# Exponent logs stacked as high and low parts on 64 contraction rows, and another round list, in an S4 block with a gated feed-forward layer

## The chip, the cores and the metric

The kernel runs on one core of one Trainium2 chip. The metric is the device time of one execution in microseconds. All numbers of the profile come from one profiled execution of the kernel before; "PE" is TensorE, "PEld" its weight loads, "ACT" ScalarE, "DVE" VectorE, "POOL" GpSimd, "SP" SyncE, which here only issues transfers.

## The reference

One layer with adaptive normalisation, of L = 2048 positions and D = 640 channels, all in float32: a state-space convolution (S4, 128 complex states per channel), then a gated feed-forward layer of width 1728.

```python
x = A_u
sa, ca, ga, sb, cb, gb = six parts of (_silu(c) @ w_mod)
h = _layernorm(x) * (1 + ca) + sa
# S4: K[d, l] = Re sum_n C[d,n] * exp(dt[d] * A[d,n] * l) * dt[d] * B[d,n],  l = 0 .. 2047
# y = causal convolution of h with K along l (by FFT of length 2 L), + h * Dskip
x = x + ga * y
h = _layernorm(x) * (1 + cb) + sb
x = x + gb * ((_silu(h @ w1) * (h @ w3)) @ w2)
```

The change is in the making of K. The exponential of a complex number times l is split: its size is exp(Re(log) * l), its direction a cosine and a sine of a phase.

## The kernel before

The convolution half takes the first 420 us or so, the feed-forward half the rest. The change touches only the convolution half, which runs in *steps* of 16 channels (40 steps, `SD = 16`). A step s goes through these parts; the names in quotes are those of the round list:

- "PH", POOL: the phases of the step, integers, one pass of 128x1024 and one of 128x512 (`ph`, L472 and L473).
- "AB", "CO", "SI", ScalarE: the absolute value of the phase (`cs<-ph`), its cosine (`cs<-cs`) and sine (`ph<-ph`), 128x1024 each.
- "PA", TensorE: the exponents Re(log) * l for the fast table, made as a matmul (`pa`, L432). The stationary side is the transposed table of logs, the moving side a constant (`r2`) that holds l in the column of its channel. 32 rows of contraction hold 32 channels; a step needs two such blocks of rows, each one matmul of 128x512 into its own PSUM bank. The product must be exact to float32, but the operands are float32r, so the table is split in a high part (`lah`) and a low part (`lal`) and two matmuls are summed: 4 a step.
- "XA", ScalarE: Exp of `pa` into the table `A` (128x1024).
- "PQ", TensorE: the same for the slow table (`pq`, L444, 128x256): `lah` and `lal` against `r1`, and the logs of the amplitude (`lmh`, `lml`) against a selection `sel`, summed: 8 a step.
- "XQ", ScalarE: Exp of `pq` into `A` (128x512).
- "E1", "E2", "A1", "A2", VectorE: exponentials times cosines (into `E`) and times sines (in `A`).
- "kg", TensorE: the kernel K of the step (`pk`, 32 small matmuls); "K", VectorE: its copy with the gate; "pt", TensorE: the first stage of its Fourier transform; "uk", ScalarE: the copy of that.

The convolution follows ten steps behind (`LAG = 10`), in chunks of 128 channels: "st", TensorE: the second stage (`p2`, shown as `p`); "kc", ScalarE: a copy of half of it; "T" and "Y", VectorE: products and sums; "iv", TensorE: the inverse stage (`pz`); "zt", ScalarE, every second step: its copy, followed by two stores from SyncE.

Three stretches set the order differently. In the *lead-in* (steps 0 to 9, with the first normalisation and the first transform of the input between them) a scheduler orders the instructions; the exponents of two steps are made in one call, `exps(s)`, and `polar` makes the tables of logs, for the first 128 channels at the start and for the other 512 during the lead-in. In the *rounds* the order is written out by hand: `ROUND` lists parts with an offset, each turn of it does four steps, and every instruction is kept in program order on its engine. `do` skips what is done already or out of range. In the rounds `pa` and `pq` share the one PSUM place "B", of one buffer. The *drain* (from `st` of step 43 on) is in program order of a plain loop.

Of the kernel before, what the change touches and what calls it, by code (L numbers as in the profile page):

```python
# [29 lines left out]
KD = D // P  # L30
# [77 lines left out]
def tile_kernel(ctx: ExitStack, tc: tile.TileContext, a):  # L108
# [9 lines left out]
    ident = cp.tile([P, P], F32, name="ident")  # L118
# [18 lines left out]
    def acopy(out, in_):  # L137
        return tc.keep_in_program_order(S.copy(out, in_))  # L138
# [31 lines left out]
    once = lambda shape, dt, name: tp.tile(shape, dt, name=name, bufs=1)  # L170
    thi = once([P, D], I32, "thi")
    phi = once([P, D], I32, "phi")
    lah = once([P, KD, P], F32R, "lah")
    lal = once([P, KD, P], F32R, "lal")
    lmh = once([P, KD, P], F32R, "lmh")
    lml = once([P, KD, P], F32R, "lml")
    r2 = once([P, NA, NB], F32R, "r2")
    r1 = once([P, NA, NA], F32R, "r1")
    sel = once([P, NA], F32R, "sel")
# [57 lines left out]
    def polar(cs, E):  # L237

        are, aim, br, bi, cr, ci = (prm[:, i, cs] for i in range(6))
        ld, dtc, m, t, g_r, g_i = (v[:, cs] for v in (ldt, dt, m0, t3, gr, gi))  # L240
        k0, nk = cs.start // P, (cs.stop - cs.start) // P

        E.tensor_tensor(g_r, br, cr, op=OP.mult)
        E.tensor_tensor(m, bi, ci, op=OP.mult)
        E.tensor_tensor(g_r, g_r, m, op=OP.subtract)
        V.tensor_tensor(g_i, br, ci, op=OP.mult)
        V.tensor_tensor(t, bi, cr, op=OP.mult)
        V.tensor_tensor(g_i, g_i, t, op=OP.add)
# [24 lines left out]

        nat = lambda v: v.rearrange("n (k p r j) -> n k r p j", k=nk, p=4, r=4)
        rows = lambda v: v[:, :nk * P].rearrange("n (k r p j) -> n k r p j", k=nk, p=4, r=4)
        for k in range(nk):
            E.tensor_tensor(rows(lt[:, 0])[:, k], nat(are)[:, k], nat(dtc)[:, k], op=OP.mult)
        for k in range(nk):
            V.tensor_tensor(rows(lt[:, 1])[:, k], nat(q)[:, k], nat(ld)[:, k], op=OP.add)
        for i, (hi, lo) in enumerate(((lah, lal), (lmh, lml))):  # L280
            pT = psS.tile([P, 2, 512], F32, name="pT", tag="AB"[i], bufs=1)
            for k in range(nk):
                PE.transpose(pT[:, 0, k * P:(k + 1) * P], lt[:, i, k * P:(k + 1) * P], ident)
            pv = pT[:, 0, :nk * P].rearrange("p (k n) -> p k n", k=nk)
            acopy(hi[:, k0:k0 + nk], pv)
            V.tensor_tensor(lo[:, k0:k0 + nk], pv, hi[:, k0:k0 + nk].bitcast(F32), op=OP.subtract)

        V.tensor_scalar(m, m, 0.5 / math.pi, 0.125, op0=OP.mult, op1=OP.add)
        V.tensor_tensor(m, m, ag, op=OP.mult)
        V.scalar_tensor_tensor(m, m, 0.25, ai, op0=OP.add, op1=OP.mult)  # L290
        V.tensor_scalar(phi[:, cs], m, TURN, 2147483520.0, op0=OP.mult, op1=OP.min)
# [124 lines left out]
    ph, cs, AA, EC, PK, K1 = {}, {}, {}, {}, {}, {}  # L416

    def exp_rows(s):
        return s // SPC, slice((s % SPC) // 2 * 8, (s % SPC) // 2 * 8 + 8), [
            (rr, slice((2 * (s % 2) + rr) * 32, (2 * (s % 2) + rr) * 32 + 32)) for rr in range(2)]  # L420

    pA, pQ = {}, {}

    def exp_fast(steps):

        for s in steps:
            pA[s] = psS.tile([P, 2, 512], F32, name="pa", tag="AB"[s % 2] if not in_order[0] else "B", bufs=1)
        for w, st in ((lah, True), (lal, False)):
            for s in steps:
                ch, js, rows = exp_rows(s)  # L430
                for rr, r in rows:
                    keep(PE.matmul(pA[s][:, rr, :], w[r, ch, :], r2[r, js, :].rearrange("p j b -> p (j b)"),  # L432
                                   start=st, stop=not st, tile_position=(r.start, 0)))

    def exp_slow(steps):

        for s in steps:
            pQ[s] = psS.tile([P, 2, 512], F32, name="pq", tag="AB"[s % 2] if not in_order[0] else "B", bufs=1)
        for i, (w, rt) in enumerate(((lah, r1), (lal, r1), (lmh, None), (lml, None))):
            for s in steps:  # L440
                ch, js, rows = exp_rows(s)
                for rr, r in rows:
                    rv = bc(sel[r, js], 2, NA) if rt is None else rt[r, js, :]
                    keep(PE.matmul(pQ[s][:, rr, :256], w[r, ch, :], rv,  # L444
                                   start=(i == 0), stop=(i == 3), tile_position=(r.start, 0)))

    def fast(s):

# [48 lines left out]
        keep(V.tensor_tensor(EC[s][:, :, 1:3, :], AA[s][:, :, 1:3, :], mid(cs[s]), op=OP.mult))  # L497

    def real2(s):
        keep(V.tensor_tensor(EC[s][:, :, 0, :], AA[s][:, :, 0, :], cs.pop(s)[:, :, 2 * NA - 1:NA - 1:-1], op=OP.mult))  # L500
# [4 lines left out]

    def imag2(s):
        A = AA[s]
        keep(V.scalar_tensor_tensor(A[:, :, 0, :], ph.pop(s)[:, :, 2 * NA - 1:NA - 1:-1], -1.0, A[:, :, 0, :],  # L508
                                    op0=OP.mult, op1=OP.mult))

    def tables(s):
# [262 lines left out]
    for tk in range(LAG):  # L774
# [748 lines left out]
```

## Time and profile before

| | us |
|---|---|
| median of 3 runs | 984.4 |
| lowest and highest run | 982.26, 985.58 |
| span of the profiled execution | 984.1 |
| busy PE, DVE, ACT, POOL in it | 918.2, 700.8, 541.1, 265.3 |
| one turn of the round list (four steps) | 28.4 |

The page gives the profiled execution by its span, first instruction to last; that is its own time here, and it lies 0.3 us under the median of the runs. A line "a:b" of the table of stages gives a stretch of the span, its length, then busy microseconds of PE, PEld, DVE, ACT and POOL with their instruction counts, the clock that the throttle granted TensorE (1.00 is full), the mean busy share of the DMA engines, and GB/s. A line of the timeline gives start, length, engine, source line, operation, tiles, count, and in brackets the idle time of the engine just before with what ended it.

### The profile page before, as it was taken

To read this page: it belongs to the slowest core of one execution; us is meant where nothing else is said; L and a number is where in the kernel's file an instruction comes from. 1 tells how busy PE (TensorE), PEld (TensorE's weight loads), DVE (VectorE), ACT (ScalarE), POOL (GpSimd) and SP (SyncE) were. 2 spreads that over 40 slices of the span, in tenths; PEclk is the share of its full clock that TensorE was granted. 3 is DMA by queue.
4 is the path that set the end of the run, shared out by engine and by line. 5 is a ranking of instruction groups with operands and counts; after the bars stand their busy time and mean duration, and the time that the engine had idled before them with its cause. 6 is when DMAs were issued, how large, how long until landed. Compare 5 with 4: busy or idle time off the path is not lost.

```text
span 984.1 us, 20582 instructions
## 1 busy us (share of the span) xinstructions
PE 918.2 (93%) x8214; PEld 687.2 (70%) x8214; DVE 700.8 (71%) x1253; ACT 541.1 (55%) x793; POOL 265.3 (27%) x274
## 2 busy tenths in 40 slices
PE   5898797989888898789999999999999999999998
PEld 2445354766666676567888888777888888888886
DVE  4598856888988886667766665568796766654575
ACT  3667665899999983246433332355753333323432
POOL 1453333444444440214422220111152222200000
PEclk9855767999999999989999999999999999999999
DMA  9463576554665587767212311896432221113443
GB/s 267 159 228 110 220 186 186 158 131 134 159 159 154 153 219 200 252 170 259 82 55 62 99 54 52 221 281 208 135 93 67 81 68 54 54 41 90 151 148 120
DMA packets 103572, 140.74 MB, mean 143 GB/s; under 512 B 20565, under 2 KB 62677, under 8 KB 103477
## 3 DMA queue, kind: packets, MB, share of 16 engines
q1 hardware_dynamic: 99668, 129.34, 45.5%
q0 software_dynamic: 2304, 7.74, 2.4%
q10 hardware_dynamic: 1504, 2.36, 0.9%
q8 instruction: 64, 1.05, 0.4%
q14 instruction: 32, 0.25, 0.1%
HBM read 107.94 MB, written 31.46 MB: 142 GB/s over the span
## 4 chain that ended last, share of the span: by engine, by line
PE 68%; ACT 15%; DVE 7%; DMA 4%; issue 3%; POOL 2%; SPq 1%; ACTq 0%; DVEq 0%; POOLq 0%
PE ps L102 52%; ACT cs L135 4%; ACT A L135 3%; ACT ph L135 3%; PE pa L432 2%; PE p L570 2%; ACT L135 2%; DMA zs<-zt 2%; PE pq L444 2%; PE pt L539 1%; PE pk L521 1%; PE pm L299 1%; DMA A<-zs 1%; PE pu L406 1%; PE pz L612 1%
## 5 line engine op out<-in xcount | busy, mean ns | idle before, releaser
L102 DVE TENSOR_TENSOR s<-ps,s 128x512 f32<-128x512 f32 x138 | 94.8, 687 | 79.8 <-PE ps L102 79.5
L472 POOL TENSOR_TENSOR ph<-thi,iota 128x1024 int32<-128x1024 int32 x40 | 85.4, 2135 | 175.1 <-DVE A L508 78.2
L102 DVE TENSOR_TENSOR gl<-rw,gh 128x640 fp32r<-128x640 f32 x87 | 78.1, 897 | 65.3 <-ACT gh L102 65.2
L102 ACT CAST gh<-rw 128x640 fp32r<-128x640 f32 x87 | 63.3, 727 | 103.9 <-PE ps L102 60.6
L570 PE MATMUL p<-uk,s 128*64 128x256 f32 x640 | 79.0, 389 | 13.3 <-PE pa L432 5.6
L102 PE MATMUL ps<-xA,gh 128*128 128x512 f32 x280 | 87.9, 392 | 0.4 <-ACT xA L102 0.4
L102 PE MATMUL ps<-gh,uh 128*128 128x512 f32 x224 | 87.5, 390 | 0.0
L102 PE MATMUL ps<-gl,uh 128*128 128x512 f32 x224 | 87.2, 389 | 0.0
L102 POOL TENSOR_TENSOR S<-rw 128x256 f32<-128x256 f32 x46 | 36.7, 799 | 174.0 <-DVE S0l L102 163.1
L102 PE MATMUL ps<-gh,ul 128*128 128x512 f32 x208 | 81.1, 390 | 0.0
L570 PEld LDWEIGHTS p<-uk,s 128*64 128x64 f32 x640 | 45.2, 138 | 38.5 <-PE pa L432 8.4
L102 PEld LDWEIGHTS ps<-xA,gh 128*128 128x128 f32 x280 | 52.1, 188 | 13.0 <-ACT xA L102 1.0
L102 PE MATMUL ps<-xA,gl 128*128 128x512 f32 x140 | 54.5, 390 | 0.0
L135 ACT ACTIVATE A<-pa 128x1024 f32<-128x1024 f32 x40 | 40.4, 1023 | 25.7 <-PE pa L432 24.3
L497 DVE TENSOR_TENSOR E<-A,cs 128x1024 f32<-128x1024 f32 x40 | 51.0, 1275 | 1.7 <-PE pk L521 1.7
L504 DVE TENSOR_TENSOR A<-A,ph 128x1024 f32<-128x1024 f32 x40 | 50.1, 1253 | 0.0
L612 PE MATMUL pz<-Y,i 64*128 64x128 f32 x640 | 45.2, 286 | 5.0 <-issue 3.1
L612 PEld LDWEIGHTS pz<-Y,i 64*128 64x128 f32 x640 | 39.1, 190 | 14.9 <-issue 11.4
L102 PEld LDWEIGHTS ps<-gl,uh 128*128 128x128 f32 x224 | 42.1, 188 | 8.9
L102 PEld LDWEIGHTS ps<-gh,uh 128*128 128x128 f32 x224 | 42.0, 188 | 8.8
L521 PE MATMUL pk<-E 128*32 128x64 f32 x1280 | 46.6, 232 | 1.2 <-DVE E L500 0.6
L539 PE MATMUL pt<-s,K 128*64 128x128 f32 x640 | 47.2, 291 | 0.5 <-ACT uk L138 0.5
(261 smaller groups left out, 2306.7 us busy)
## 6 DMA issues: line engine op xcount, KB each, us to landing
rw<-in_w_dram SPq DMA_DIRECT2D x52, 320.0 KB
us<-u SPq DMA_DIRECT2D x16, 640.0 KB
s<-in_s_dram SPq DMA_DIRECT2D x40, 256.0 KB
i<-in_i_dram SPq DMA_DIRECT2D x40, 256.0 KB
rw<-in_wg_dram SPq DMA_DIRECT2D x31, 320.0 KB
rw<-in_wu_dram SPq DMA_DIRECT2D x28, 320.0 KB
uk<-us SPq DMA_DIRECT2D x32, 256.0 KB
zs<-zt SPq DMA_DIRECT2D x32, 256.0 KB
```

The lines of the kernel that those rows point to most:

```text
L102: ins = fn(*args, **kw)
L135: return tc.keep_in_program_order(S.activation(*args, **kw))
L299: PE.matmul(pm[g, :n], scb[:, k], w[:, k, :], start=(k < 4), stop=(k > 0), tile_position=(0, g.start))
L432: keep(PE.matmul(pA[s][:, rr, :], w[r, ch, :], r2[r, js, :].rearrange("p j b -> p (j b)"), start=st, stop=not st, tile_position=(r.start, 0)))
L444: keep(PE.matmul(pQ[s][:, rr, :256], w[r, ch, :], rv, start=(i == 0), stop=(i == 3), tile_position=(r.start, 0)))
L472: hold(G.tensor_tensor(p, bc(thi[:, sl], 2, NPH), bc(iota, 1, SD), op=OP.mult))
L497: keep(V.tensor_tensor(EC[s][:, :, 1:3, :], AA[s][:, :, 1:3, :], mid(cs[s]), op=OP.mult))
L504: keep(V.tensor_tensor(A[:, :, 1:3, :], A[:, :, 1:3, :], mid(ph[s]), op=OP.mult))
L521: keep(PE.matmul(pk[dq * 32:dq * 32 + 32, g, :], x[:, g * 4 + dq, 1, :], x[:, g * 4 + dq, 0:3:2, :], start=(st == 0), stop=(st == 1), tile ...
L539: keep(PE.matmul(pt[c * 64:c * 64 + 64, g, :], kk[:, g, :], s1[:, c, :], start=True, stop=True, tile_position=(0, c * 64)))
L570: keep(PE.matmul(p2[par * 64:par * 64 + 64, pi, c, :], s2[:, pi * 2 + par, c * 64:c * 64 + 64], uk[:, 0:kn + 1:kn, f, :], start=True, stop ...
L612: ins = keep(PE.matmul(pz[:, par, (g % 2) * 2 + pi, :], i1[r, pi, c, :], Y[r, pi, c, :], start=(c == 0), stop=(c == 1), tile_position=(par ...
```

## The change

Three edits.

1. The tables of logs. `lah` and `lal` become one table `la`, whose 64 rows of a block hold the high parts of 32 channels and below them the low parts of the same 32; `lm` likewise. The split is made before the transpose: ScalarE casts the logs to the high part, VectorE subtracts, both into `l2` (a piece of the room `uk` that also holds other early values and, later, loaded weights), and twice as many 128x128 blocks are transposed, then copied by ScalarE. The adds and products ahead of it go in halves of 64 columns.
2. The matmuls. One matmul with 64 rows of contraction takes the place of two with 32: 2 `pa` and 4 `pq` a step in place of 4 and 8. A step's two row blocks are rows 0 to 63 and 64 to 127. A call for two steps now does one step after the other.
3. The round list is another one, and runs three turns more, skipping what is done; the plain loop after it starts at step 36 and skips likewise.

```diff
-    lah = once([P, KD, P], F32R, "lah")
...
+    la = once([P, 2 * KD, P], F32R, "la")
+    lm = once([P, 2 * KD, P], F32R, "lm")
...
-        for i, (hi, lo) in enumerate(((lah, lal), (lmh, lml))):
-            pT = psS.tile([P, 2, 512], F32, name="pT", tag="AB"[i], bufs=1)
-            for k in range(nk):
-                PE.transpose(pT[:, 0, k * P:(k + 1) * P], lt[:, i, k * P:(k + 1) * P], ident)
-            pv = pT[:, 0, :nk * P].rearrange("p (k n) -> p k n", k=nk)
-            acopy(hi[:, k0:k0 + nk], pv)
-            V.tensor_tensor(lo[:, k0:k0 + nk], pv, hi[:, k0:k0 + nk].bitcast(F32), op=OP.subtract)
+        for i, dst in enumerate((la, lm)):
+            raw = lt[:, i, :nk * P].rearrange("n (b c) -> n b c", c=32)
+            both = l2[:, :2 * nk * P].rearrange("n (b s c) -> n b s c", s=2, c=32)
+            acopy(both.bitcast(F32R)[:, :, 0], raw)
+            V.tensor_tensor(both[:, :, 1], raw, both[:, :, 0], op=OP.subtract)
+            pT = psS.tile([P, 2, 512], F32, name="pT", tag="AB"[i], bufs=1).rearrange("p a b -> p (a b)")
+            for k in range(nt):
+                PE.transpose(pT[:, k * P:(k + 1) * P], l2[:, k * P:(k + 1) * P], ident)
+            acopy(dst[:, 2 * k0:2 * k0 + nt], pT[:, :nt * P].rearrange("p (k n) -> p k n", k=nt))
...
-        for w, st in ((lah, True), (lal, False)):
-            for s in steps:
...
+            t, js, rows = exp_rows(s)
+            for rr, r in rows:
+                keep(PE.matmul(pA[s][:, rr, :], la[r, t, :], r2[r, js, :].rearrange("p j b -> p (j b)"),
+                               start=True, stop=True, tile_position=(r.start, 0)))
...
-        for i, (w, rt) in enumerate(((lah, r1), (lal, r1), (lmh, None), (lml, None))):
...
+            for i, w in enumerate((la, lm)):
                 for rr, r in rows:
...
+        "A1+0 pt-2 K-1 st+1 CO+1 E1+1 iv-1 uk-2 pt-1 kc+1 zt-1 kg+0 PH+4 T+1 CO+2 uk-1 E2+1 Y+1 SI+1 E1+2 "
...
-    for rnd in range(NS // EB):
+    for rnd in range(NS // EB + 3):
...
-    for tk in range(NS + 1, LAG + 8 * NDC + 2):
+    for tk in range(NS - 4, LAG + 8 * NDC + 2):
```

What the change does to the order is seen best where the exponents are made. First ScalarE before, from a turn's table load of Exp on (`A<-pa` and `A<-pq` are the Exps, the number tells the step apart):

```order
L135 ACT_TABLE_LOAD
L135 ACTIVATE A_2965<-pa_2934 128x16x2x32
L138 COPY kc_2968<-p2_2950 128x512
L135 ACTIVATE A_2965<-pq_2970 128x16x32
L135 ACTIVATE A_3034<-pa_2996 128x16x2x32
L138 COPY uk_82<-pt_2980 128x32x16
L135 ACTIVATE A_3034<-pq_3043 128x16x32
L138 COPY zt_3065<-pz_2858 128x2x4x128
L135 ACTIVATE cs_3073<-ph_2894 128x1024
L135 ACTIVATE A_3090<-pa_3075 128x16x2x32
L138 COPY kc_3094<-p2_3054 128x512
L138 COPY uk_82<-pt_3081 128x32x16
```

The same place on ScalarE after the change:

```order
L135 ACT_TABLE_LOAD
L135 ACTIVATE A_2820<-pa_2745 128x16x2x32
L138 COPY kc_2843<-p2_2825 128x512
L135 ACTIVATE A_2820<-pq_2838 128x16x32
L138 COPY uk_82<-pt_2759 128x32x16
L135 ACTIVATE A_2853<-pa_2846 128x16x2x32
L138 COPY zt_2855<-pz_2750 128x2x4x128
L135 ACTIVATE A_2853<-pq_2895 128x16x32
L135 ACTIVATE cs_2919<-ph_2900 128x1024
L135 ACTIVATE A_2921<-pa_2913 128x16x2x32
L135 ACTIVATE cs_2938<-ph_2935 128x1024
L135 ACTIVATE A_2921<-pq_2941 128x16x32
```

The `uk` copy has moved between the first step's second Exp and the second step's first one, where nothing stood; `zt` has moved into the second step, and a `cs` into the third.

TensorE before, at the first exponents of the same turn:

```order
L432 MATMUL pa_2934<-r2_98,lah_94 128x512 x2
L432 MATMUL pa_2934<-r2_98,lal_95 128x512 x2
L570 MATMUL p2_2950<-uk_82,s2_2948 64x256 x8
L444 MATMUL pq_2970<-r1_99,lah_94 128x256 x2
L444 MATMUL pq_2970<-r1_99,lal_95 128x256 x2
L444 MATMUL pq_2970<-sel_100,lmh_96 128x256 x2
L444 MATMUL pq_2970<-sel_100,lml_97 128x256 x2
L539 MATMUL pt_2980<-s1_73,K1_2939 64x128 x8
L432 MATMUL pa_2996<-r2_98,lah_94 128x512 x2
L432 MATMUL pa_2996<-r2_98,lal_95 128x512 x2
```

TensorE after, at the same exponents (this turn's first `pa` now stands further ahead):

```order
L609 MATMUL pz_2750<-Y_2713,i1_2805 128x128 x8
L567 MATMUL p2_2825<-uk_82,s2_2823 64x256 x8
L441 MATMUL pq_2838<-r1_97,la_94 128x256 x2
L441 MATMUL pq_2838<-sel_98,lm_95 128x256 x2
L431 MATMUL pa_2846<-r2_96,la_94 128x512 x2
```

`pt` no longer stands between a step's `pq` and the next step's `pa`, and each block has half its rows.

More of the change, by code (lines that the diff above doesn't have):

```diff
@@ L172, in tile_kernel @@
     phi = once([P, D], I32, "phi")
-    lah = once([P, KD, P], F32R, "lah")
-    lal = once([P, KD, P], F32R, "lal")
-    lmh = once([P, KD, P], F32R, "lmh")
-    lml = once([P, KD, P], F32R, "lml")
+    la = once([P, 2 * KD, P], F32R, "la")
+    lm = once([P, 2 * KD, P], F32R, "lm")
     r2 = once([P, NA, NB], F32R, "r2")
@@ L197, in tile_kernel @@
     ldt, dt, m0, t3, gr, gi = (flat[2][:, i * D:(i + 1) * D] for i in range(6))
+    l2 = flat[2][:, 4 * D:4 * D + 2 * (D - DC)]
     def w_load(w, c0):
@@ L272, in polar @@
         yield
-        nat = lambda v: v.rearrange("n (k p r j) -> n k r p j", k=nk, p=4, r=4)
-        rows = lambda v: v[:, :nk * P].rearrange("n (k r p j) -> n k r p j", k=nk, p=4, r=4)
-        for k in range(nk):
+        nt = 2 * nk
+        nat = lambda v: v.rearrange("n (t p r j) -> n t r p j", t=nt, p=4, r=2)
+        rows = lambda v: v[:, :nk * P].rearrange("n (t r p j) -> n t r p j", t=nt, p=4, r=2)
+        for k in range(nt):
             E.tensor_tensor(rows(lt[:, 0])[:, k], nat(are)[:, k], nat(dtc)[:, k], op=OP.mult)
-        for k in range(nk):
+        for k in range(nt):
             V.tensor_tensor(rows(lt[:, 1])[:, k], nat(q)[:, k], nat(ld)[:, k], op=OP.add)
-        for i, (hi, lo) in enumerate(((lah, lal), (lmh, lml))):
-            pT = psS.tile([P, 2, 512], F32, name="pT", tag="AB"[i], bufs=1)
-            for k in range(nk):
-                PE.transpose(pT[:, 0, k * P:(k + 1) * P], lt[:, i, k * P:(k + 1) * P], ident)
-            pv = pT[:, 0, :nk * P].rearrange("p (k n) -> p k n", k=nk)
-            acopy(hi[:, k0:k0 + nk], pv)
-            V.tensor_tensor(lo[:, k0:k0 + nk], pv, hi[:, k0:k0 + nk].bitcast(F32), op=OP.subtract)
+        for i, dst in enumerate((la, lm)):
[4 more added lines that the diff above has]
+            pT = psS.tile([P, 2, 512], F32, name="pT", tag="AB"[i], bufs=1).rearrange("p a b -> p (a b)")
+            for k in range(nt):
+                PE.transpose(pT[:, k * P:(k + 1) * P], l2[:, k * P:(k + 1) * P], ident)
+            acopy(dst[:, 2 * k0:2 * k0 + nt], pT[:, :nt * P].rearrange("p (k n) -> p k n", k=nt))
         V.tensor_scalar(m, m, 0.5 / math.pi, 0.125, op0=OP.mult, op1=OP.add)
@@ L418, in exp_rows @@
     def exp_rows(s):
-        return s // SPC, slice((s % SPC) // 2 * 8, (s % SPC) // 2 * 8 + 8), [
-            (rr, slice((2 * (s % 2) + rr) * 32, (2 * (s % 2) + rr) * 32 + 32)) for rr in range(2)]
+        return s // 4, slice(s % 4 * 8, s % 4 * 8 + 8), [(rr, slice(rr * 64, rr * 64 + 64)) for rr in range(2)]
     pA, pQ = {}, {}
@@ L427, in exp_fast @@
             pA[s] = psS.tile([P, 2, 512], F32, name="pa", tag="AB"[s % 2] if not in_order[0] else "B", bufs=1)
-        for w, st in ((lah, True), (lal, False)):
-            for s in steps:
[L430 to L433, printed above, removed]
+            t, js, rows = exp_rows(s)
+            for rr, r in rows:
+                keep(PE.matmul(pA[s][:, rr, :], la[r, t, :], r2[r, js, :].rearrange("p j b -> p (j b)"),
+                               start=True, stop=True, tile_position=(r.start, 0)))
     def exp_slow(steps):
@@ L438, in exp_slow @@
             pQ[s] = psS.tile([P, 2, 512], F32, name="pq", tag="AB"[s % 2] if not in_order[0] else "B", bufs=1)
-        for i, (w, rt) in enumerate(((lah, r1), (lal, r1), (lmh, None), (lml, None))):
-            for s in steps:
-                ch, js, rows = exp_rows(s)
+            t, js, rows = exp_rows(s)
+            for i, w in enumerate((la, lm)):
                 for rr, r in rows:
-                    rv = bc(sel[r, js], 2, NA) if rt is None else rt[r, js, :]
-                    keep(PE.matmul(pQ[s][:, rr, :256], w[r, ch, :], rv,
-                                   start=(i == 0), stop=(i == 3), tile_position=(r.start, 0)))
+                    keep(PE.matmul(pQ[s][:, rr, :256], w[r, t, :], bc(sel[r, js], 2, NA) if i else r1[r, js, :],
+                                   start=(i == 0), stop=(i == 1), tile_position=(r.start, 0)))
     def fast(s):
@@ L499, in real2 @@
     def real2(s):
-        keep(V.tensor_tensor(EC[s][:, :, 0, :], AA[s][:, :, 0, :], cs.pop(s)[:, :, 2 * NA - 1:NA - 1:-1], op=OP.mult))
+        keep(V.tensor_tensor(EC[s][:, :, 0, :], AA[s][:, :, 0, :], cs[s][:, :, 2 * NA - 1:NA - 1:-1], op=OP.mult))
     def imag1(s):
@@ L507, in imag2 @@
         A = AA[s]
-        keep(V.scalar_tensor_tensor(A[:, :, 0, :], ph.pop(s)[:, :, 2 * NA - 1:NA - 1:-1], -1.0, A[:, :, 0, :],
+        keep(V.scalar_tensor_tensor(A[:, :, 0, :], ph[s][:, :, 2 * NA - 1:NA - 1:-1], -1.0, A[:, :, 0, :],
                                     op0=OP.mult, op1=OP.mult))
@@ L826, in tile_kernel @@
     ROUND = (
[5 rows of a table removed]
[5 rows of a table added]
     ).split()
     in_order[0] = True
-    for rnd in range(NS // EB):
+    for rnd in range(NS // EB + 3):
         for word in ROUND:
             name, k = word[:2].rstrip("+-"), EB * rnd + int(word[len(word[:2].rstrip("+-")):])
+            if all((n, NS - 1) in done for n in parts) or (name in conv and k > NS + 1):
+                continue
             do(name, k)
@@ L839, in tile_kernel @@
                 x_load((k - 24) // 2)
-            if name == "kg" and 36 <= k < 40:
+            if name == "kg" and 36 <= k < NS:
                 early.append((None, z_tile()))
```

9 rows, old and new, of the table ROUND are left out of this document.

## The prediction

> **What bounds the kernel now.** I read the page first, for where the time is and whose chain it is; then a table of stages; then, in the stage of the change, the waits of ScalarE and the instructions in order of time.
>
> ```profile
> span 984.1 us, 20582 instructions
> PE 918.2 (93%) x8214; PEld 687.2 (70%) x8214; DVE 700.8 (71%) x1253; ACT 541.1 (55%) x793; POOL 265.3 (27%) x274
> ```
>
> TensorE at 93% is an average over different stages. The feed-forward half (from about 425 us) keeps it full and has no exponent matmul in it. The change lies in the first 420 us, so I cut those into stages: two of the scheduled lead-in, the turns of the round list (each from the exponent matmul `pa` of step 4r to that of step 4r+4; the first and the last of five full ones stand here, one more goes before them), and the drain.
>
> ```profile
> 50.00:100.00 50.00, 44.15 (x454) 23.13 (x457) 44.32 (x75) 35.17 (x43) 21.54 (x21) 0.54 0.50 172
> 100.00:169.06 69.06, 57.52 (x833) 32.67 (x821) 48.30 (x83) 43.03 (x52) 23.69 (x16) 0.72 0.64 188
> 197.02:225.46 28.44, 25.66 (x503) 18.73 (x496) 24.50 (x40) 26.42 (x33) 12.98 (x9) 1.00 0.58 152
> ...
> 310.51:338.87 28.36, 25.64 (x503) 18.73 (x498) 24.49 (x40) 26.35 (x33) 12.98 (x9) 1.00 0.57 150
> 367.20:420.00 52.80, 43.67 (x616) 29.77 (x608) 35.74 (x77) 16.52 (x29) 7.34 (x13) 0.96 0.77 229
> ```
>
> After the length come busy PE, weight loads, VectorE, ScalarE, GpSimd, then the granted clock. The five turns take 141.85 us (197.02 to 338.87), 28.37 each. ScalarE is busy some 26.35 us of one, PE 25.65, VectorE 24.5: three engines close together, ScalarE first. So a turn is ScalarE's work plus what ScalarE waits, some 2.0 us. The waits, over the five turns from 197.02 to 338.87:
>
> ```profile
> ACT A L135 <- PE pa L432: 5.4, 5, 1.1
> ACT A L135 <- PE pq L444: 3.4, 10, 0.3
> ```
>
> All of them (8.8 us, 1.76 a turn) are for the exponent matmuls. One pair of steps in order of time:
>
> ```profile
> 255.15 0.68 DVE L500 TENSOR_TENSOR E<-A,cs 128x512 f32<-128x512 f32 x1
> 255.75 1.21 DVE L497 TENSOR_TENSOR E<-A,cs 128x1024 f32<-128x1024 f32 x1
> 256.89 1.21 DVE L504 TENSOR_TENSOR A<-A,ph 128x1024 f32<-128x1024 f32 x1
> 256.94 1.02 ACT L135 ACTIVATE A<-pa 128x1024 f32<-128x1024 f32 x1
> 257.86 0.58 ACT L138 COPY kc<-p 128x512 f32<-128x512 f32 x1
> 258.01 0.39 PE L444 MATMUL pq<-r,lah 32*128 32x256 f32 x2 [0.73 <-ACT A L135]
> 258.02 0.68 DVE L508 SCALAR_TENSOR_TENSOR A<-ph,A 128x512 f32<-128x512 f32 x1
> 258.23 0.28 PE L444 MATMUL pq<-r,lal 32*128 32x256 f32 x2
> 258.35 0.27 PE L444 MATMUL pq<-sel,lmh 32*128 32x256 f32 x2
> 258.46 0.27 PE L444 MATMUL pq<-sel,lml 32*128 32x256 f32 x2
> 258.63 0.68 DVE L587 TENSOR_TENSOR T<-p,kc 128x512 f32<-128x512 f32 x1
> 258.66 1.09 PE L539 MATMUL pt<-s,K 128*64 128x128 f32 x16
> 258.78 0.60 ACT L135 ACTIVATE A<-pq 128x512 f32<-128x512 f32 x1 [0.34 <-PE pq L444]
> 259.69 0.50 PE L432 MATMUL pa<-r,lah 32*128 32x512 f32 x2
> 260.02 0.40 PE L432 MATMUL pa<-r,lal 32*128 32x512 f32 x2
> 260.07 0.42 DVE L594 TENSOR_TENSOR Y<-T,p 128x256 f32<-128x256 f32 x1
> 260.35 0.32 PE L521 MATMUL pk<-E 128*32 128x64 f32 x8
> 260.46 1.02 ACT L135 ACTIVATE A<-pa 128x1024 f32<-128x1024 f32 x1 [1.08 <-PE pa L432]
> ```
>
> The exponents' PSUM place has one buffer in the rounds, so this is a ping-pong: matmul `pa`, Exp on ScalarE, matmul `pq`, Exp, the next `pa`. What ScalarE has between two Exps decides whether it waits. Here a `kc` copy covers part of `pq` (0.34 us stay open), and nothing stands between the second Exp and the next first one, with `pt` ahead of `pa` on PE besides: 1.08 us open.
>
> **The change part by part.**
>
> *Half the matmuls in a round.* A `pq` block is four pairs, 0.65 us to the next instruction (258.01 to 258.66). Two pairs stay: the first takes 0.22 to its successor, the last 0.20, so 0.42; 0.23 less. A `pa` block is 0.66 (259.69 to 260.35); one pair stays, 0.33; 0.33 less. That is 0.56 a step, 2.24 a turn on PE, which falls from 25.65 to about 23.4. Since PE isn't the bound this counts only through the ping-pong: Exp to Exp over `pq` falls from 1.84 (256.94 to 258.78) to 1.61; over `pa`, with no `pt` between, the gap becomes 0.60 (the Exp) + 0.05 + 0.44 (0.77 from `pa` to its Exp, less 0.33), 1.09. That two pairs of 64 rows run side by side as those of 32 rows do is not shown by a `pa` row; if they did not, a `pa` block would stay near 0.66 and the gap at 1.42.
>
> *The order of ScalarE in a round.* New order from the table load: Exp, `kc`, Exp, `uk`, Exp, `zt`, Exp, `cs`, Exp, `cs`, Exp, `kc`, `uk`, Exp, `cs`, Exp. Every gap now has a cover. By starts in the trace, Exp to what follows is 0.92 (256.94 to 257.86), and the other steps come from one turn earlier:
>
> ```profile
> 233.95 0.60 ACT L135 ACTIVATE A<-pq 128x512 f32<-128x512 f32 x1 [0.34 <-PE pq L444]
> 234.44 1.01 ACT L138 COPY zt<-pz 128x1024 f32<-128x1024 f32 x1
> 235.33 1.07 ACT L135 ACTIVATE cs<-ph 128x1024 f32<-128x1024 int32 x1
> 237.87 0.60 ACT L138 COPY uk<-pt 128x512 f32<-128x512 f32 x1
> ```
>
> A short Exp takes 0.49 to the next start, `zt` 0.89; `uk` ends 0.60 and `cs` 1.07 after it starts. Now the gaps. First `pq`: covered to 0.92 + 0.58 = 1.50, wanted 1.61, idle 0.11. First `pa`: covered to 0.49 + 0.60 = 1.09, wanted 1.09, idle up to 0.05. Second `pq` under `zt`: 0.92 + 1.01 = 1.93, covered, though `pk` now stands ahead of that `pq`. Third `pa` under `cs`: 0.49 + 1.07 = 1.56, covered. Third `pq`: `p` (1.95 us) now stands ahead of it on PE, wanted 2.09, covered to 1.99, idle 0.10. The fourth pair lies under `kc`, `uk` and `cs`. Sum 0.26, so a turn is 26.35 + 0.26 = 26.6 us, 1.75 less.
>
> *What else must fit into 26.6.* PE 23.4 and VectorE 24.5 do, but no longer with much to spare. From the end of a turn's first cosine (1.2 us after the table load) VectorE has twelve pieces in a row. By the steps in the fence: two wide E (1.14 each), two narrow E (0.60), one wide A (1.13), two narrow A (0.61), two products (1.44), one `K` (about 0.55) and two sums (about 0.7), 10.7 us, so it ends near 12.0. Only then may `p` of the turn's third convolution step run: it writes the PSUM place that those sums read, and takes about 1.95. Its `kc` copy stands on ScalarE behind four cosines (estimated at 1.05 each, 0.95 for a sine or Abs: a step is 0.1 less than the length, as for the Exp), five sines or Abs, four short copies (0.48), a `zt` (0.89), the table load (1.29) and the first Exp (0.92): 4.2 + 4.75 + 1.9 + 0.9 + 1.3 + 0.9 = 14.0. And 12.0 + 1.95 = 13.95: it just fits. If VectorE falls behind by d, `kc` and the `pq` behind it move by d, in every turn. That is the bad end of this term: d = 1 leaves 0.75 a turn. The good end is no wait at all: 28.37 less the sum of ScalarE's start-to-start steps over a turn (25.8 us by the same estimates), 2.55.
>
> How often: six turns from 169.06 to 338.87, and the last four Exp pairs (to 355.9), which hold all of a turn's waits again: seven times. 7 x 1.75 = 12.2; ends 5 and 18. The table loads stay two a turn. The copies and transfers moved on ScalarE and SyncE (`zt` with its two stores, `uk`, `kc`) keep their place within a turn; POOL's passes for a table still end before its `cs`, though the tightest by under 1 us.
>
> *The lead-in.* Here two steps are computed together:
>
> ```profile
> 72.92 0.80 PE L432 MATMUL pa<-r,lah 32*128 32x512 f32 x2 [0.65 <-DVE u L412]
> 73.51 0.63 PE L432 MATMUL pa<-r,lal 32*128 32x512 f32 x2
> 74.07 0.33 PE L521 MATMUL pk<-E 128*32 128x64 f32 x3
> ...
> 136.99 0.80 PE L432 MATMUL pa<-r,lah 32*128 32x512 f32 x4
> 137.58 0.64 PE L432 MATMUL pa<-r,lal 32*128 32x512 f32 x4
> 138.15 1.33 PE L299 MATMUL pm<-uk,scb 128*32 128x384 f32 x4
> ```
>
> Four tiles of 32 rows took 1.16 us (136.99 to 138.15), no longer than two (72.92 to 74.07): side by side they already cost half. Two steps as two 64-row pairs one after the other then save nothing; only blocks of a single step do, 0.57 each. I count four such `pa` blocks (2.3 us), and by the same reasoning some 2.5 us of `pq`. Against it stand ten more transposes, and two casts, a wider copy and a subtraction per table ahead of them:
>
> ```profile
> 107.79 0.94 PE pT L283 x4
> ```
>
> Four took 0.94. At 0.235 us each that is 2.35, and the chain to the first tables gets about 1.5 longer (my estimate: a cast and a subtraction of about 0.6 each and a wider copy). Net 4.8 - 2.35 - 1.5 = 1 us less. VectorE is as busy as PE here (44.32 against 44.15 of 50), so PE's saving may not show, and the scheduler has put this part in another order: ends 5 us better and 5 worse.
>
> The clock is the unknown here: 0.54 and 0.72 granted in these stages with PE 88% and 83% busy, and 1.00 in the rounds at 90%. The Trainium skill ("TensorE: Matmul & The Clock Gate", Part 1) has the clock at full speed after one busy window of about 3.4 us, and at half only after an idle one. The trace does not follow it: nearly the same busy share gets 0.54 in one place and 1.00 in another. By that rule the rounds stay at full clock, since their longest PE gap stays near 1 us, and the clock rival below would fall away and its chance go to the forecast; by the rows it stays.
>
> *The drain.* The same pieces remain after the last Exp, with one `pt` and one `uk` more and one VectorE piece less; 0, give or take 1.5.
>
> Sum: 984.1 - 12.2 - 1 = 971 for the profiled execution; its span is 0.3 under the median of the runs (984.4), so **971.5 us**.
>
> **The rivals.**
>
> *Everything on the path (0.12).* ScalarE runs back to back and the lead-in gives its 5 us: 984.4 - 18 - 5 = 961. For it: the 25.8 us of ScalarE steps. Against it: VectorE's 24.5 in the same turn.
>
> *A new wait for the old one (0.12).* The chain cosine, VectorE, `p`, `kc` is late by d = 1 to 1.7, and a turn ends at 27.6 to 28.3: 984.4 - 7 x 0.05 to 0.75 - 1, that is 978 to 983. The list leaves this chain no slack. Against it: VectorE's busy time is 24.50 and 24.49 in the first and the last turn, so its steps hardly vary. A 64-row pair that is not concurrent belongs here: 0.33 more at the first `pa` gap, some 2.5 us in all, 974.
>
> *Slower: the granted clock (0.08).* Fewer exponent matmuls could lower what the throttle grants. If the rounds got the lead-in's 0.72, PE would need 23.4 / 0.72 = 32.5 us a turn, 4.1 more than now, 984.4 + 7 x 4.1 = 1013; it decides from a clock of 23.4 / 28.36 = 0.82 down. Only in the lead-in, at 0.60 in place of 0.72, the 57.52 us would become 69, up to +11: 984.4 - 12.2 + 11 = 983, no gain. Against it: a 64-row matmul fills as much array as two of 32 rows, so the rounds get denser; and the drain, 83% busy, has 0.96.
>
> **How the numbers follow.** The forecast has 0.68: 966 to 977 by its own ends. 0.3% of 984, 3 us, is about what the measurement can tell from no change. Range 961 to 982: it leaves out the clock case, and the outer edges of the others, together under 0.2. Faster: 0.68 + 0.12 + 0.04 (the near part of the new wait) = 0.84; same: 0.07 (its far part); slower: 0.09 (the clock, and 0.01 for a far part with a bad lead-in).
>
> **What would show it.** Right: turns of 26.4 to 26.9 us with ScalarE busy 26.3 in each; the 1.08 us wait for `pa` gone; `pq` blocks of two pairs about 0.42 us long; PE 23.4 a turn; clock 1.00; the first Exp of step 12 near 171 us as now. Wrong: turns above 27.5, with `kc` waiting for `p` and `p` for `Y`; a clock under 0.95 between 170 and 340; a lead-in that ends more than 5 us off.

## The result, and the profile after

| | before | after |
|---|---|---|
| median, us | 984.78 (20 runs) | 984.56 (20 runs) |
| lowest and highest | 980.2, 988.64 | 979.96, 992.09 |
| ratio, 95% interval | | 1.0002 (0.9983 to 1.0021) |
| span of the profiled execution | 984.1 | 986.7 |
| one turn of the round list | 28.37 | 28.72 |

No change that can be measured, where 12 to 13 us less were forecast. The page after:

```profile
span 986.7 us, 20165 instructions
PE 897.5 (91%) x7984; PEld 675.2 (68%) x7984; DVE 719.0 (73%) x1259; ACT 545.4 (55%) x797; POOL 275.3 (28%) x278
```

TensorE is busy 20.7 us less, and VectorE, whose work in the rounds was not changed, 18.2 us more. The table of stages after, cut as before at the first `pa` of step 4r (length, then busy PE, PEld, DVE, ACT, POOL, clock):

```profile
50.00:100.00 50.00, 39.72 (x436) 19.30 (x431) 43.32 (x78) 38.44 (x46) 25.13 (x26) 0.61 0.45 169
100.00:167.95 67.95, 52.75 (x718) 29.29 (x706) 48.72 (x88) 42.21 (x50) 22.42 (x16) 0.78 0.65 194
167.95:194.03 26.08, 21.42 (x443) 15.61 (x441) 24.54 (x37) 23.19 (x29) 10.88 (x6) 1.00 0.57 166
222.76:251.45 28.69, 23.49 (x474) 17.54 (x472) 27.12 (x41) 27.60 (x34) 14.15 (x8) 1.00 0.53 148
251.45:280.13 28.68, 24.75 (x475) 18.62 (x473) 27.25 (x41) 25.42 (x32) 14.15 (x8) 0.94 0.51 142
308.88:337.62 28.74, 24.82 (x475) 18.55 (x473) 27.72 (x41) 25.43 (x32) 14.15 (x8) 0.94 0.50 137
```

PE is at the 23.4 a turn that was forecast (23.49 at full clock), the lead-in ends 1.1 us sooner, but the turns are 28.7 us, and VectorE is busy 27.1 to 27.7 of each of the three full ones shown (the last three rows), with about as many instructions as before (41 against 40). These three have the same length at a clock of 1.00 and of 0.94. ScalarE's waits over the five turns from 194.03 to 337.62:

```profile
ACT cs L135 <- POOL ph L470: 4.3, 5, 1.1
ACT A L135 <- PE pq L441: 2.4, 5, 1.2
ACT kc L138 <- PE p L567: 2.2, 5, 0.8
```

The wait for `pa` is gone, as forecast. In its place ScalarE waits for GpSimd's phases, and `kc` for `p`. The wait for `pq` is 0.5 us a turn, where 0.2 was forecast: TensorE keeps its order, and `pk`, ahead of that `pq`, waits 9.2 us in the five turns for VectorE's `K`. VectorE's groups by form, in the five turns before and then after (`L497` and `L500` of before are `L494` and `L497` of after):

```profile
L497 DVE TENSOR_TENSOR E<-A,cs 128x1024 f32<-128x1024 f32 x20 | 24.3, 1217 | 0.0
L500 DVE TENSOR_TENSOR E<-A,cs 128x512 f32<-128x512 f32 x20 | 13.7, 683 | 0.0
```

```profile
L494 DVE TENSOR_TENSOR E<-A,cs 128x1024 f32<-128x1024 f32 x20 | 29.1, 1456 | 3.9 <-ACT cs L135 3.9
L497 DVE TENSOR_TENSOR E<-A,cs 128x512 f32<-128x512 f32 x20 | 24.5, 1224 | 0.0
L584 DVE TENSOR_TENSOR T<-p,kc 128x512 f32<-128x512 f32 x20 | 13.6, 682 | 1.5 <-ACT kc L138 1.5
```

The same products of the same shapes take 1456 ns in place of 1217, and 1224 in place of 683: (29.1 - 24.3 + 24.5 - 13.7) / 5 = 3.1 us more a turn. Nothing else on VectorE grew. The timeline shows what lies beside the long ones:

```profile
261.31 1.05 POOL L470 TENSOR_TENSOR ph<-ph,phi 128x512 int32<-128x512 int32 x1
261.77 1.15 DVE L497 TENSOR_TENSOR E<-A,cs 128x512 f32<-128x512 f32 x1
264.57 1.21 DVE L494 TENSOR_TENSOR E<-A,cs 128x1024 f32<-128x1024 f32 x1
264.79 2.75 POOL L469 TENSOR_TENSOR ph<-thi,iota 128x1024 int32<-128x1024 int32 x1 [2.43 <-DVE A L505]
265.71 2.39 DVE L497 TENSOR_TENSOR E<-A,cs 128x512 f32<-128x512 f32 x1
267.62 1.37 POOL L470 TENSOR_TENSOR ph<-ph,phi 128x512 int32<-128x512 int32 x1
```

The two engines take turns (the profile gives GpSimd's times only roughly). `E` of 261.77 does not end until 0.56 after GpSimd's pass has ended (262.36). The pass of 264.79 finds a wide `E` running, ends 1.76 after that has ended (265.78), and holds up the narrow `E` of 265.71 meanwhile, which ends 0.56 after it. A blocked instruction is not shown as waiting but as long. In the order before, the same passes fell mostly on other work: over the five turns they lay beside an `E` for 8.1 of their 65.2 us, in the new order for 30.5 of 71.2 (added up from the timelines). One pass before:

```profile
258.63 0.68 DVE L587 TENSOR_TENSOR T<-p,kc 128x512 f32<-128x512 f32 x1
258.85 1.91 POOL L472 TENSOR_TENSOR ph<-thi,iota 128x1024 int32<-128x1024 int32 x1 [3.56 <-DVE A L508]
259.34 0.70 DVE L588 TENSOR_TENSOR p<-p,kc 128x512 f32<-128x512 f32 x1
```

`T` has `p` in PSUM as one of its operands, and neither side is slowed. A pass starts when the last `A` product of four steps earlier frees its buffer (`[... <-DVE A L508]`; `ph` has four). So the order of VectorE's pieces behind that `A` decides what a pass meets: in the old list mostly T, Y and K, which read PSUM, or an `E` that has just begun and is waited for; in the new one an `E` lies in the way of most narrow passes and of some wide ones.

The Trainium skill ("SBUF — State Buffer", section "Who interferes with whom") says that a VectorE instruction with two SBUF inputs contends with a GpSimd instruction that reads SBUF, not with one that only writes, and that one with at most one SBUF input, outside the two-port modes, does not contend. The rows above agree with the first and the last; the middle was still to be tried.

### The profile page after: what moved, and what is told of

It is laid out like the page before. It is cut to its first block, busy times and chain, and to the rows that moved or that the text cites. A ratio compares the mean times of both kernels' runs of the same rounds, so it can differ in the third digit from the quotient of the medians.

```text
span 986.7 us, 20165 instructions
## 1 busy us (share of the span) xinstructions
PE 897.5 (91%) x7984; PEld 675.2 (68%) x7984; DVE 719.0 (73%) x1259; ACT 545.4 (55%) x797; POOL 275.3 (28%) x278
## 4 chain that ended last, share of the span: by engine, by line
PE 67%; DVE 17%; ACT 7%; DMA 4%; issue 3%; SPq 1%; POOL 0%; ACTq 0%; DVEq 0%; POOLq 0%
PE ps L102 54%; DVE E L494 3%; DVE E L497 3%; PE p L567 2%; PE pk L518 2%; DMA zs<-zt 2%; PE pz L609 2%; ACT cs L135 1%; PE pt L536 1%; DVE p L585 1%; DVE A L501 1%; ACT ph L135 1%; DVE T L584 1%; DVE A L505 1%; PE pu L408 1%
## 5 line engine op out<-in xcount | busy, mean ns | idle before, releaser
L102 DVE TENSOR_TENSOR s<-ps,s 128x512 f32<-128x512 f32 x138 | 94.9, 688 | 79.9 <-PE ps L102 79.6
L494 DVE TENSOR_TENSOR E<-A,cs 128x1024 f32<-128x1024 f32 x40 | 56.1, 1402 | 5.9 <-ACT cs L135 5.2
L518 PEld LDWEIGHTS pk<-E 128*32 128x32 f32 x1280 | 32.9, 117 | 30.5 <-DVE K L526 17.3
L470 POOL TENSOR_TENSOR ph<-ph,phi 128x512 int32<-128x512 int32 x40 | 51.7, 1292 | 4.0 <-DVE phi L293 1.0
L102 ACT ACTIVATE s<-ps 128x512 f32<-128x512 f32 (+1 forms) x33 | 19.7, 597 | 51.5 <-PE ps L102 51.5
```

Source lines behind the costliest of these rows:

```text
L102: ins = fn(*args, **kw)
L470: keep(G.tensor_tensor(p[:, :, :NA], p[:, :, :NA], bc(phi[:, sl], 2, NA), op=OP.add))
L518: keep(PE.matmul(pk[dq * 32:dq * 32 + 32, g, :], x[:, g * 4 + dq, 1, :], x[:, g * 4 + dq, 0:3:2, :], start=(st == 0), stop=(st == 1), tile ...
```

## The experiments

Theory A is this exclusion. The rivals were B, the clock (it is 0.94 in three of the five turns, though these are no longer than the two at 1.00), and C, the chain cosine, VectorE, `p`, `kc`, which the prediction had as a rival. Turns are read from the profiled execution, between the first `pa` of steps 4r.

**Each half alone.** e1 is the changed kernel with the old list:

> The changed kernel with the round list (and its loop) of before: edits 1 and 2 alone. Theory A (VectorE's products E, A with two operands in SBUF and GpSimd's passes shut each other out; in the new list they fall on each other, in the old list seldom): turns 27.7 to 28.1 us (28.37 less the shorter pa and pq blocks), VectorE's wide E near 1.22 and narrow E near 0.70 us a piece, total 979 to 982. Theory B (a slower or throttled clock of the 64-row matmuls holds the turn): turns 28.4 to 28.8 with a clock under 0.97 in the rounds, total 983 to 986. Theory C (the new order's chain cosine, VectorE, p, kc has no slack, whatever GpSimd does): as A here.

e2 is the kernel before with the new list:

> The kernel before with the new round list and loop: edit 3 alone, with 32-row matmuls. Theory A: the list alone makes the turn, since VectorE with GpSimd's passes on top sets it and the exponents have room: 28.6 to 28.9 us, VectorE's wide E 1.4 to 1.5 and narrow E 1.1 to 1.3 us; total 984 to 988. Theory B (the 64-row matmuls lower the clock): clock 1.00 and turns under 28.4, total 980 to 984. Theory C: turns 28.6 to 29.2, with E at 1.22 and 0.68.

e1 took 987.48 us (ratio to before 1.0024, 0.9991 to 1.0056), e2 985.25 (0.9996, 0.9978 to 1.0015): neither half gains. Two turns of e1, one of e2:

```profile
223.71:251.66 27.95, 23.55 (x478) 17.55 (x472) 24.79 (x40) 26.16 (x33) 12.89 (x9) 1.00 0.53 135
251.66:281.30 29.64, 25.15 (x479) 18.36 (x472) 24.66 (x40) 27.93 (x35) 14.37 (x10) 0.94 0.59 163
```

```profile
219.42:247.95 28.53, 25.54 (x498) 18.99 (x497) 27.43 (x41) 26.57 (x33) 14.16 (x8) 1.00 0.51 140
```

In the old list the smaller matmuls give 0.4 us a turn at full clock (28.37 to 27.95), but in two of five turns the clock falls to 0.94 and the turn is 29.64. In the new list VectorE is as long with 32-row matmuls (27.4 us, `E` 1532 and 1224 ns) as with 64, and the turn is 28.53 at full clock throughout: the list makes the long turn, not the clock. In e1 `E` is at 1216 and 684 ns. A has e1's turn right at full clock; e2's lies 0.07 us under what A gave. The total of e1 is 5 us above what A gave, by those slow turns among others.

**GpSimd out of the way.** e3 leaves its passes away from step 13 on:

```diff
-        act(c, ph[s], AF.Abs)
+        act(c, ph[s] if s < 13 else bc(thi[:, s * SD:s * SD + SD], 2, NPH), AF.Abs)
```

(the sine likewise, and `phases` makes only the tile)

> The changed kernel without GpSimd's phase passes from step 13 on: absolute value and sine read the row of increments in their place, so the phases of those steps are left out. Theory A: E back at 1.22 and 0.68 us, VectorE busy 24.4 a turn, turns 26.3 to 26.8, total 966 to 972. Theory B: turns stay at 28.4 to 28.8 with the clock at 0.94 to 1.00 by turns. Theory C: E back at its length but turns 28 or more, with kc waiting for p.

e4 keeps them as passes that only write:

```diff
+        if s >= 13:
+            keep(G.memset(p.bitcast(F32), 0.0))
+            keep(G.memset(p[:, :, :NA].bitcast(F32), 0.0))
...
+            return
```

> The changed kernel with GpSimd's two phase passes from step 13 on replaced by two passes that write the same tile and read nothing (fill with zero), so the phases of those steps are left out; every wait of the phases on GpSimd stays. Theory A in the form that only GpSimd's reading shuts VectorE's second operand out: E at 1.22 and 0.68 us, turns 26.3 to 26.9, total 966 to 973. If any GpSimd pass shuts it out: E between 1.25 and 1.4, turns 27 to 28.2. If it is the wait for the phases (cs waits for GpSimd) and not the length of E: turns 27.5 to 28.5 with E short.

e9 makes each fill twice, so that GpSimd is as long as with its own passes:

> As e4 (the changed kernel, GpSimd's phase passes from step 13 on replaced by fills, so the phases of those steps are left out), but each fill is made twice, so that GpSimd is as long on a table as its two reading passes alone are: 2 x 0.95 + 2 x 0.53 = 2.95 us against 1.90 + 1.05. Theory A in the form that only GpSimd's reading shuts VectorE out: 26.5 to 26.8 us a turn, E at 1.22 and 0.68 us, total 966 to 973. If e4 was quick because its passes were short and the cosine waited less: 27 to 28.7 us.

e3 took 971.59 us (ratio 0.9859, 0.9796 to 0.9921), e4 969.44 (0.9837, 0.9793 to 0.9881), e9 970.82 (0.9857, 0.9827 to 0.9887), with two runs each. A turn of e3, then of e9:

```profile
220.69:247.25 26.56, 23.32 (x475) 17.55 (x474) 24.19 (x41) 26.18 (x33) 0.00 (x0) 1.00 0.56 150
```

```profile
189.39:215.97 26.58, 23.34 (x474) 17.55 (x472) 24.17 (x41) 26.19 (x33) 11.83 (x16) 1.00 0.60 160
```

The turn is 26.56 us in e3 and e4 and 26.58 in e9, VectorE 24.2, the clock 1.00 in all five turns, wide `E` 1219 to 1221 ns and narrow `E` 681 to 684 in all three, and in e3 and e4 the view of waits has no row for ScalarE. In e9 GpSimd is busy 11.83 us a turn, as long as its four pairs of reading passes when nothing blocks them (4 x 2.95), and 17.5 us of its fills in five turns lie beside an `E`; the timeline of e9:

```profile
254.93 1.21 DVE L499 TENSOR_TENSOR E<-A,cs 128x1024 f32<-128x1024 f32 x1
255.13 3.13 POOL L470 MEMSET ph<- 128x1024 f32 x4 [1.86 <-DVE A L510]
256.06 0.68 DVE L502 TENSOR_TENSOR E<-A,cs 128x512 f32<-128x512 f32 x1
```

Nothing is stretched. So a GpSimd pass that reads shuts out VectorE's second SBUF operand and a fill does not, as the section cited above says; B and C fall, since the list, the matmuls and the length of GpSimd's work are the same. A fill differs from the passes in its operation too, and a pass with one input was not tried. In these three kernels the sines and cosines are not the true ones; that it isn't the data is shown by e6 below, which computes the true ones and takes 26.77 us a turn.

**Longer products or late cosines?** GpSimd is held up too, so its phases come later, and the cosine with them. e10 lets the absolute value read the increments from step 13 on (the first line of e3's edit) and leaves GpSimd as it is:

> The changed kernel with GpSimd's reading passes as they are, but from step 13 on the absolute value reads the row of increments and not the phases (so the cosines of those steps are left out): the exclusion stays, the wait of the cosine for GpSimd goes. It tells whether the turn is longer by VectorE's longer pieces or by the late cosine. If VectorE's pieces alone make it: E still 1.35 to 1.5 and 1.0 to 1.25 us, VectorE busy over 26.5 a turn, turns 27.8 to 28.7, total 978 to 985. If the late cosine makes it: turns 26.6 to 27.4 with E still long, total 968 to 975.

It took 985.08 us (ratio 0.9999, 0.9978 to 1.002), turns 28.69 on the mean of five:

```profile
218.96:247.70 28.74, 23.47 (x474) 17.55 (x472) 27.07 (x41) 27.54 (x34) 14.16 (x8) 1.00 0.52 143
```

ScalarE no longer waits for GpSimd, `E` is at 1500 and 1225 ns, and the turn is as long: the late cosine doesn't set it, the longer products do. (ScalarE's wait for `pq` has grown in its place, from 2.4 to 5.0 us in five turns.)

**The old list without the exclusion.** e11 is e1 with the fills of e4:

> e1 (64-row matmuls, old list) with GpSimd's phase passes from step 13 on replaced by fills (the phases of those steps are left out). Theory A says that in the old list, too, GpSimd shuts out some of VectorE's pieces (wide A at 1.30 us in e1) and holds back the cosine: turns 27.2 to 27.6 at full clock where e1 has 27.95. If the old list is held by the order of ScalarE's copies alone: 27.9 to 28.0.

980.23 us (ratio 0.9956, 0.993 to 0.9983); turns 27.27 on the mean of five, at full clock. The old list pays some 0.7 us a turn for it as well.

**One word of the list.** e5 moves `E1+4` away from where GpSimd starts:

```diff
-  ... PA+6 Y+3 AB+5 ... PA+7 E1+4 E2+4 PH+7 ...
+  ... PA+6 E1+4 Y+3 AB+5 ... PA+7 E2+4 PH+7 ...
```

> The changed kernel with one word of the round list moved: E1+4 goes from behind A2+3 to fifteen words earlier, between PA+6 and Y+3, so that GpSimd, which A2+3 releases, finds one narrow E in its way and then K and T (which have an operand in PSUM), where it found a wide and a narrow E. Theory A (two-operand products in SBUF and GpSimd's reads shut each other out): about 1 us a turn less, 27.4 to 28.0 us, VectorE's wide E down from 1456 to 1250 to 1350 ns or narrow E from 1224 to 850 to 1050 ns; total 976 to 980. Theory C (the wait of kc for p and p for Y): E1 ahead of Y+3 makes Y, p and kc later by 1.2 us, so turns of 28.7 to 29.9, total 985 to 993.

982.54 us (ratio 0.9983, 0.9958 to 1.0009); four turns of five took 28.45 us, not 27.4 to 28.0 (the first took 28.08). VectorE by form over four turns:

```profile
L494 DVE TENSOR_TENSOR E<-A,cs 128x1024 f32<-128x1024 f32 x16 | 24.8, 1550 | 6.0 <-ACT cs L135 4.7 <-PE pk L518 1.0 <-ACT A L135 0.3
L505 DVE SCALAR_TENSOR_TENSOR A<-ph,A 128x512 f32<-128x512 f32 x16 | 14.0, 878 | 0.0
L497 DVE TENSOR_TENSOR E<-A,cs 128x512 f32<-128x512 f32 x16 | 10.9, 679 | 0.0
```

The narrow `E` is back at 679 ns, but the passes now fall on the wide `E` (1550) and the narrow `A` (878). VectorE is still busy 26.3 us of a turn, and wide `E` waits 1.2 us a turn for the cosine (4.7 / 4), which waits for GpSimd. One word moves the collision; it doesn't remove it. My expectation missed.

**A list written around it.** e6 has another order of the same words, written so that GpSimd's reading passes meet few products from SBUF. e7 is another such list; this is e6's:

```diff
+  "PA+4 K+0 PH+4 zt-1 uk-1 E2+1 A2+1 E1+2 st+2 SI+3 SI+2 iv+0 A1+1 AB+4 E2+2 kg+1 kc+2 pt+0 T+2 Y+2 "
+  "iv+1 st+3 CO+3 SI+4 CO+4 A1+2 XA+4 kc+3 E1+3 PQ+4 XQ+4 K+1 PA+5 uk+0 A2+2 XA+5 E2+3 PH+5 T+3 zt+1 "
+  "kg+2 PH+6 PQ+5 Y+3 pt+1 XQ+5 AB+5 A2+3 PA+6 st+4 XA+6 K+2 E1+4 AB+6 A1+3 PQ+6 iv+2 XQ+6 PA+7 PH+7 "
+  "E2+4 uk+1 pt+2 kc+4 XA+7 uk+2 PQ+7 XQ+7 T+4 CO+5 CO+6 kg+3 Y+4 st+5 kc+5 K+3 iv+3 A1+4 A2+4 AB+7 "
+  "E1+5 T+5 kg+4 Y+5 pt+3 SI+5 "
```

> The changed kernel with a round list written so that GpSimd's passes fall on VectorE's pieces that read PSUM (K, T, Y) or on the ends of other pieces, with the same parts and the same 64-row matmuls. Theory A: turns 26.3 to 26.9 us, VectorE busy under 25.5 a turn, total 968 to 974, the gain that was forecast for the change. If the exclusion is only part of it: 27 to 28, total 975 to 981.

> As the run before it, with another such list, which keeps more of the order of the kernel before. Theory A: turns 26.3 to 26.9 us, total 968 to 974.

e6 took 971.32 us (ratio 0.985, 0.9825 to 0.9876), e7 971.9 (0.9853, 0.982 to 0.9885). e6 ran once more, as e12:

> The kernel of e6 again, in five rounds, for a narrower interval: total 969 to 973, ratio to before 0.983 to 0.988, turns 26.77 us as in e6.

972.27 us (ratio 0.987, 0.984 to 0.9901). Turns: 26.77, 26.78 and 26.77 us on the mean of five. e6, a turn, two groups, and one GpSimd pass in the timeline:

```profile
210.05:236.81 26.76, 23.72 (x474) 17.19 (x472) 25.73 (x41) 26.23 (x33) 13.66 (x9) 1.00 0.59 156
```

```profile
L501 DVE TENSOR_TENSOR A<-A,ph 128x1024 f32<-128x1024 f32 x20 | 27.6, 1378 | 0.0
L497 DVE TENSOR_TENSOR E<-A,cs 128x512 f32<-128x512 f32 x20 | 13.7, 683 | 0.0
```

```profile
248.72 0.69 DVE L497 TENSOR_TENSOR E<-A,cs 128x512 f32<-128x512 f32 x1
248.95 2.22 POOL L469 TENSOR_TENSOR ph<-thi,iota 128x1024 int32<-128x1024 int32 x1 [3.50 <-DVE A L505]
249.32 0.68 DVE L584 TENSOR_TENSOR T<-p,kc 128x512 f32<-128x512 f32 x1
250.04 0.70 DVE L585 TENSOR_TENSOR p<-p,kc 128x512 f32<-128x512 f32 x1
```

The pass waits out the end of one product and then lies under the two products of T, `p` among their operands, and the first sum of Y. VectorE still loses some (wide `A` 1378 ns): it is busy 25.73 us a turn, where under 25.5 was expected, but it has room for that in 26.77. This is 1.3 to 1.5% less than the kernel before, and than the changed one, which takes as long; from the changed one it differs in the order alone.

**What the matmuls are worth there.** e8 is e6's list with 32-row matmuls:

> The list of e6 with the 32-row matmuls and tables of the kernel before. It tells what the matmuls are worth once GpSimd is out of VectorE's way. By the ping-pong of the exponents (0.33 us more a pa block, 0.23 a pq block, four of each a turn): turns 27.8 to 28.6 us, so the halving is worth 1.4 to 2.2 us a turn here and nothing in the list of the change; total 979 to 985. If the matmuls hide behind other work: 26.4 to 27.0, total 970 to 975.

It took 992.77 us (ratio 1.007, 1.0045 to 1.0094). Two neighbouring turns:

```profile
189.44:217.87 28.43, 25.91 (x498) 18.84 (x496) 25.82 (x41) 26.57 (x33) 13.66 (x9) 1.00 0.57 149
217.87:247.68 29.81, 27.32 (x498) 20.01 (x497) 25.82 (x41) 26.65 (x33) 13.66 (x9) 0.94 0.53 141
```

The turn at full clock is as expected: ScalarE waits 7.6 us for `pq` and 3.6 for `pa` in the five turns, in e6 0.2 for both. The total is 8 us above, since two turns of five ran at 0.94 (29.8 us), and for more that the profiled execution (span 985.0) doesn't show. At full clock, then, in us a turn (new list with 64 rows: the mean of five, alike at both clocks):

| list | 32 rows | 64 rows |
|---|---|---|
| old | 28.37 | 27.95 |
| new | 28.53 | 28.72 |
| e6 | 28.44 | 26.77 |

Halving the matmuls is worth 0.4 in the old list, nothing in the new one, and 1.7 in a list in which VectorE has room. In the totals it brought no gain in the old list (e1), and between e8 and e6 it is 20 to 21 us; some 6 us of that are in neither the turns nor their clock, and stay open.

## Why the prediction was wrong

- *The turn by ScalarE's order, 26.6 us: right for what it counted.* Without GpSimd's reads the new list runs at 26.56: 26.18 of ScalarE and 0.38 of gaps too short to be listed as waits, where 26.35 and 0.26 were forecast. In the changed kernel, too, a `pq` block takes 0.42 to 0.43 us to the next instruction and a `pa` block 0.33 to 0.43, where 0.42 and 0.33 were forecast. The rival "everything on the path" (25.8 a turn) falls: with no wait of ScalarE listed, the turn is 26.56.
- *The step that failed: "PE 23.4 and VectorE 24.5 do" fit.* VectorE's 24.5 was read in the old order and taken along as if it belonged to the work. It belongs to the work and to what GpSimd does meanwhile. The new list moved GpSimd's passes under the `E` products, which added 3.1 us a turn. So VectorE has 26.8 to 27.7 us, 27.2 on the mean, and with what it waits for `cs` and `kc` ((3.9 + 1.5) / 5 = 1.1) and 0.4 of short gaps the turn is 28.7. In the old list the prediction's 24.5 holds (24.7 to 25.1 in e1); it is the new list that it was wrong for.
- *"POOL's passes still end before their `cs`": wrong too.* ScalarE waits 4.3 us in five turns for them. e10 shows that this did not set the turn.
- *A sign stood in the trace of before.* GpSimd's wide pass took 1.91 us at 258.85, where it lay beside T, and over 2.2 on the mean; 3.56 us of idle ahead of it said that it starts when an `A` ends. Both concern a step that the new list moves, and the prediction looked at it only for its own due time.
- *The rival "a new wait for the old one"* had the right engine late and `kc` waiting for `p` (2.2 us in five turns), but by another cause, and its 978 to 983 was just too low: VectorE's pieces got longer, not only its margin used up.
- *The rival of the clock* is not the cause: e2 has 1.00 and nearly the same turn. But the rounds do not stay at full clock, as the rule cited from the Trainium skill ("TensorE: Matmul & The Clock Gate", Part 1) would have it: three of five turns have 0.94, and in e1 and e8 such turns cost 1.4 to 1.7 us each, in the changed kernel nothing. The prediction's "their longest PE gap stays near 1 us" failed as well: TensorE waited up to 2.1 us for `K` here (268.69 is one such place), since `K` comes behind the stretched `E`.
- *The lead-in, -1:* 167.95 against 169.06 looks right, but can't be told. With the same list and lead-in the first `pa` of step 12 came at 164.21 in e10 and at 169.84 in e3.
- *The first turn, 26.08 us,* looks like the forecast and isn't: it has 29 ScalarE instructions where later ones have 32 to 34.
- *The drain, 0:* from the first `pa` of step 36 to the end before took 984.1 - 338.87 = 645.2, after 986.7 - 337.62 = 649.1. With the new list and no exclusion it is 645.1 (e4) to 646.7 (e3). Up to the end of the last `zt` the stretch is 79.1 before, 81.6 after, and 79.8 and 79.9 in e3 and e4, so some 1.7 us of this are the exclusion in the last turns as well; the rest lies in the feed-forward half, where single executions differ by as much.
- *A slip in the sum:* 984.1 - 12.2 - 1, with the 0.3 added, is 971.2 and not 971.5. It changes nothing.

## What to carry to other kernels

An engine's busy time is not a property of its work when a neighbour shares its port: before reordering, list the VectorE instructions with two SBUF operands and the GpSimd instructions that read SBUF, and look at which of them meet in the new order. The profile shows such blocking as longer instructions, not as waits, so compare the mean duration of each form, not only the table of waits. A halved cost on one engine can be worth nothing until another is given room: here 1.7 us a turn or nothing, by the order alone.

## What the runs showed of the hardware

- The blocked side keeps its place. When GpSimd's pass waited for a VectorE product, it got the port at that product's end, ahead of VectorE's next one (264.79 to 267.54), and then the second pass in turn waited for VectorE (267.62).
- Writing and reading differ: GpSimd's fills of 128x1024 (0.95 us each) slowed no product, its reading passes of 1.90 us did.
- The clock falls by a fixed piece. Turns with 0.94 were 1.69 (e1) and 1.38 us (e8) longer than their neighbours; 0.06 of 29.64 us is 1.8 us lost, which is 3.6 us at half speed. The table of stages, cut finer, shows it: in e1 the clock is 0.50 from 274.68 to 278.10 and 1.00 on both sides, one piece of 3.41 us. The Trainium skill ("TensorE: Matmul & The Clock Gate", Part 1) has windows of about 3.4 us and half speed after an idle one; the length agrees, while the window ahead was not idle here, as the last lines of this point show. TensorE in e1 at the same place in two turns:

```profile
245.74 1.95 PE L567 MATMUL p<-uk,s 128*64 128x256 f32 x16 [1.97 <-issue]
...
273.77 2.83 PE L567 MATMUL p<-uk,s 128*64 128x256 f32 x16 [1.96 <-ACT uk L138]
```

  Two waits of the same length, shorter than such a window; after one the 16 matmuls take 1.95 us, after the other 2.83. The changes of the clock lie on a grid of 3.41 us, and the wait falls differently on it. In the grid piece ahead of a slow one TensorE was busy 0.37 to 0.42 of the time (in e1 1.45 of 3.41 us, from 271.27 on): so at all eight slow pieces in the rounds of the changed kernel, e1 and e10. After pieces of 0.48 or more the clock stayed at 1.00, from 172 to 360 us of every run but e8. There it fell after 0.66 and 0.68, with no wait over 1.24 us ahead, and not after 0.64, so the busy share alone is not the rule. No run was made to try it.
